# A new global order, new engines and new buffer homes for all 1,263 tasks of a linear-attention and expert-attention kernel

## The chip, the cores and the metric

The kernel runs on one core of one Trainium2 chip. The metric is device time in microseconds (us) of that core, as the median of three runs. The profile comes from one further execution of the same program.

## The reference

Two stages follow each other. The first is linear attention per head with a normalised output; the second is a small mixture of four attention experts on that output.

```python
# stage 1: q, k, v are (8, 8, 576, 64): batch, heads, sequence, head size
kv  = einsum('bhsd,bhse->bhde', k, v)
out = einsum('bhsd,bhde->bhse', q, kv)
rms = sqrt(mean(out * out, axis=-1) + 1e-06)
x   = (out / rms * g_norm)            # regrouped to (8, 576, 512)

# stage 2: 4 experts, 2 chosen per token, head size 64
logits = x @ w_gate                   # (512, 4)
w      = softmax over the two largest logits of a token
for e in range(4):
    q, k, v = x @ wq[e], x @ wk[e], x @ wv[e]
    a  = softmax(causal(q @ k.T / 8))
    ye = a @ v @ wo[e]
    out += (w of expert e, 0 where it isn't chosen) * ye
```

Inputs and output are float32; 28.3 MB of q, k and v are read and 9.4 MB are written.

## The kernel before

The program is a flat list of 1,263 tasks. A task is named by a kind, a batch b (0 to 7) and one or two part numbers: `("sc", 3, 1, 2)` is the third piece of scores of expert pair 1 in batch 3, written `sc.3.1.2` below. Each task calls one small function that issues one to a few dozen instructions. `names()` lists all tasks, `ORDER` is a string with two characters for each task that says in which order they are issued, and `ENGINE` has one letter for each task: A (ScalarE, called ACT), V (VectorE, DVE) or G (GpSimd, POOL), used where a task can run on more than one engine. Every engine takes its own tasks strictly in that order, so the order decides what stands behind what in five queues: TensorE (PE), DVE, ACT, POOL, and the queue of SP that issues nearly all DMAs. Batch 0's v is issued by ACT.

`SLOTS` gives each buffer a home, in the order of first use. There are 8 homes of kind L (a whole k, v, q or turned q of one batch, 9.2 KB in each partition, named `kvq` in the profile), 13 of kind t (`tmp`: raw weights, gate products, x before its transpose, y before its store), and 8 PSUM banks (all named `p` in the profile). A PSUM tile is either one bank (`small`) or a pair of banks (`big`). A task that writes into a home waits for the last reader of the buffer that was there before.

The tasks of a batch b are, in the order in which data flows:

| kind | engine | what it does |
|---|---|---|
| lk, lv, lq (lkr, lvr) | SP | loads of k, v, q (and of the last 64 tokens of k and v). Batches 0 and 1 come in halves of 576 KB; batches 2 to 7 as 1,024 KB each for k and v and eight pieces of 144 KB for q |
| q, then qc | PE, DVE or ACT | transposes of q on PE for batches 0 and 1; for batches 2 to 7 qc is a DVE transpose (L478) |
| kv, kvr, kvc | PE, DVE or ACT | k times v, and its copy out of PSUM into `kvx` |
| kgm, kgr | POOL or DVE, DVE | the gate's columns added to `kvx` (L450, L457) |
| out, oc | PE, ACT or DVE | q times `kvx`, and the copy to `o_sb` |
| sq, red, ln, rs, na, nb, nc | POOL or ACT, DVE, ACT, ACT, DVE, DVE or POOL, DVE | squares (L506, L508), their sum, and 1/rms with a Newton step |
| xm | DVE or POOL | scales `o_sb` by 1/rms into `tmp` (L564) |
| x, xc | PE, ACT or DVE | transposes x into `xT` |
| gl, lg, m8, sh, ex, mk, gt, den, rd, gate | DVE, POOL, ACT | the gate of every token |
| qp, kp, qpc, kpc, v, vc | PE, then ACT or DVE | the projections and their copies |
| sc, exp, msk | PE, ACT, POOL | scores, exponentials (L690), causal mask (L696) |
| pv, rc, iv, oc2 | PE, DVE, DVE or POOL, DVE | a times v, and the scaling |
| ot, otc, y, yc, st | PE, ACT or DVE, PE, ACT or DVE, SP | transpose, the product with wo, copy, store (L781) |

Five prologue tasks belong to batch 0 alone: gg and gb broadcast g_norm and w_gate over the partitions by matmul on PE, g8, g9 and wg scale them on DVE; lw, ws and lwo, wo load and scale the weights.

L276 is the one line of a helper through which every matmul goes, and L285 that of every copy, so the profile's groups are told apart by their tiles.

`ZEROS` asks for matmuls of zeros (`p<-zeros`) ahead of a task: they are issued just before it, into the bank that it will write, and are overwritten by it. In the kernel before there are 69 of them at 18 tasks, from batch 0 to batch 7.

Of the kernel before, what the change touches and what calls it, by code (L numbers as in the profile page):

```python
# [20 lines left out]
DIGITS = "0123456789ABCDEFGHIJKLMNOPQRSTUVWXYZabcdefghijklmnopqrstuvwxyz+-"  # L21

ZEROS = {
    ('kv', 0, 1): 9, ('kv', 0, 0): 9, ('out', 0, 0): 6, ('out', 0, 1): 2, ('out', 0, 3): 6,
    ('kv', 1, 1): 3, ('x', 0, 1): 6, ('kv', 2, 0): 2, ('sc', 0, 0, 1): 2, ('y', 0, 3): 2,
    ('out', 2, 3): 6, ('x', 1, 2): 2, ('sc', 1, 1, 0): 2, ('ot', 1, 1): 2, ('ot', 2, 0): 2,
    ('sc', 3, 1, 1): 4, ('x', 4, 1): 2, ('sc', 7, 1, 2): 2,
}

ORDER = (  # L30
    "050104030M02305I00060908072+310c0A0B0e0d0a0G0E0N0b0f0C0T0I2-0V0Y5N0Z0K0S0U0Q0W5P0X0H5K0g0F0w0h0D0i0x0J0k0j0o0l"
    "320p0+0m0-0q0n0s0O130y0L0r5O140t0z7l18340u100R115G19150v1I1J161A1D171K1E1S1L1F1M1T125H1b3C1U0P1P1o7q3D1c2z1p1G"
    "3E1B1C1H1V1d1Q1R5F3F1N1W1Y1u7m1m1v1X1Z1n1O1q1a1e3A1h1r1f7n1g1i2M1j3B1k1l7f1y2N2K1z1s2L1w1t331x5Q2R35242SAA2O38"
    "1+39362527AD28262P5R375T2T1-5S2Q5U295V203G7g3W3H2U3X3I2V2X7j2Y212W3J5L5W222Z2a5X2b5e5M5Y2c3O2f5f3K3P235Z5a2A3L"
    "3Q2C3M2d2D2eA93N2B2E3Y7r2F5J3R7t2G5b7sA47u2H2g3Z2I3S2h2JA62i3T2j7h3U2t2n2u7k3V2q2o7i2k5c3a2r2w2l3b3c2x3d5d2m3e"
    "3h5s5g2s5k3n2y3i3f3j5h3k2v3o2p3g423q3wA35l3p3lAE435m815w3tAC3m7v5n7w5t3x46805i7xCZ445x473r3y7+455y3u5j3s5o5z3v"
    "5u485p4e493z5q7-3+4C3-5r4f7p405v414A4D7y4E5+4B5-CW607z4c4FCV61AF4dAICT62AH65A8AGA54G6E4M4H4J666H7o4K4P636B4Q4N"
    "4gCa4m674L4h4O6C646S6K6D4I6F4i6T4n4S686G6WA76I4U6X4o6Y6J694RAB6Z6L6a4V6A6N4W4T6M6b6O6UCU4X6P6e4Y6Q826RCd4Z726V"
    "6fCe4a8373704bE-6c71776d7478AJ8GAK75Ez794pASChALAT764q8HCiAMEvAQCfCgAR4rE+4jAOAN6jEt4k6gCjCkAP6h4lEy88896i6pEu"
    "6q8A4s6k4t4u4v7D4x6lHR7A8B7E6r7B7F6m4w4y4z6n7C4+844-8C6o85Ex8K8D5686Cl8L6s57598MCb8E7G6u875A537I506v8I8FCm5C54"  # L40
    "6w6t5D51Co7H6xCnAk5B7L8JAU6y7J6z557K6+7M5E8NF36-F57N8OCp8P527O8QCc7PFFF658F48RFECY7c7Z8S7dCX8T7T8b7a7Q7U7W7e8h"
    "7R8c7X8U8V8d7V8iAl7b8w8jCs8YAV7Y8W8k8x7SAc8XAW8eAYEwAdAXAgAeAZ8+F0Ah8ZAfHNAa8fF18a8-8sCr8gAi8u8tAb8y8v8n928lAm"
    "Aj8mF28zAn8o9S938pCtAoHPAp8q90Cq9T8rAqArHQ9QAs91Av94HI9RA-9DF89EF795D0AyHSCyF9D8B5HO9U9VAtFG96HK9FD9Cz9W9XD1B2"
    "9aAu9A9YFH9dFAB89BAzB0HL9Z9eA+9bB69CB1HMB39fC+BIB79cB4BKBJHJB99gD2C-BABM9iBLDA9h9jBNFCHHAw9k979lAxDBCu9m98BB9n"
    "D4BCHh9oCv99BOBDD59pBSCwBEBPFBBFBQD3BTHgBsBRCxFD9HD6BtHf9GBG9L9I9MBq9J9NBH9KBdBUBrBeBaBVBf9OD7BXHe9PHTBWHVBYA0"
    "HUA1BbHWBZA29zDCBc9wDD9+9t9xDE9-BgDFDG9u9qDH9yDPBh9r9vBu9sBlBxDSBiDIBvDQDYHXBjDRHYBmBkBwFIHZDJBnByDkBoDTDVDlFJ"
    "BpDKDUB+DLBzC1FUB-DMFYFVC2C0FZDmDgC3DnHaC4DhDWC6C5DXC7HbFKDNDoC8DOC9DZFQDpHcDaFLFMFRDsFNCAHdFSFWCBEGFOFXDtFPCC"
    "EHDiFTFaDqCDDjFbCNDrCKDbCODcFcCEFdCLDdCHFeCPDeFfDfEECFCICMFgCGFjCQEFCJE1DuFsE2EIDvELFkFhEJCRFmFtFlCSEMFuD+DwEO"
    "EKFiGAD-FpFyFnGBG4EPENFoFqE0G5ERFrDxEQG6DyFzG8FvEUF+ESG9HuEWG7DzHmETHvEXHyE3HnF-EYEVG0HzHoG1E4G2EZFwE6E5G3HpFx"
    "EaE7HiEbH+E8HqHjE9H-GGHrHkHsGCGHHlGgGDHwEAHtEcGhGeEBEdHxECGfGEEDI0I1I2EnI3GFEhI4I7EoEeEiEkEpIAEfEqEjGLElGREgI8"  # L50
    "IDGMEmIBGSIGI9GlGiErIEGjICEsGNIHIJIFIUGmIWIIGkIYIVGTIXGnIaIZI5IKIbI6GIILGrGOGJIMJ6IPINGsGKGPIcGtJ7IgIOGQIdIeIQ"
    "IhIRISITGVIfJ4GZGaGbGUJ5IrGoGWIsGXJ8GpGYItJBGcJ9GqIoGdIlIpJAIiIjIqGuGvGwImGxGyIkJHGzG+JIG-InJCJEJJH0IvJFH1JDIu"
    "IzHBI+IwI-H8JGHCH5H9IxHDJKIyH6H2HAJMJNJLJOH7J2H3J0JSJ3J1HEJPJTH4JQHFJWJRHGJZJXJUJcJaJVJYJfJdJbJiJgJeJjJhJk"
)
ENGINE = (
    "VVVVVVVVVVVVVVVVVGVGVGVGVAVVVVAVVVGVVAVVVVVAAVVAGVVVGVVAAVVVAVAAVGVAAVVVAAVGVAAVGVAAVVVGVVVAVVAVVVGVAVVAVGAVVV"
    "VVVAVVVVVVVAVAVVVAGVAGVAGVAGVVVVVVGVVAVAVAVAGVAGVAGVAGVVVVVVVVVVVVVVAVVAVVAVVVVVVVVVVVVVGVVVVAVAVVVVGVVAAVVAAV"
    "VAGVVVGVAAVGVVVVVAGVAVVVGVAGVAVGAVGVVGVAVVVVVAVVVAVVVAGVAGVAGVAGVVVVVVGVVVVVVAVAGVAGVAGVAGVVVGVVGVVVVVVVAVVVVV"
    "AVVAVVVVVVVVVVVVVVVVVVVVGVGVVVVVVVGVVAAVVVAVVAGVVAAVAAVVVVVVVVGVAVVAVVVVVAVGAVGVVGVVVVVVVVVVVAVVVAGVAGVAGVAGVV"
    "VGVVVVVAVVVAVAGVAGVAGVAGVVVVVVVVVAVAVVAVVAVVAVVAVVVVVVVVVVVVVVVVVVVAVVGVVVVVVVGVVAGVVAGVVAAVVAAVAAVVVVVGVVGVAV"  # L60
    "VAGVAVVAVVAVGVVVVAVAVAVAVVVAVAVAGVAGVAGVAGVVVVVVVVVAVAVAVAGVAGVAGVAGVVVGVVGVVAVAVVAVVAVVAVVVVVVVVVVVVVVVVVVVVV"
    "VAGVGVVVVVVAAVVVGVVAAVVAGVVVAVAAVVVVVVVAVVVVVVGVVVVVVGAVGVVVVVVAVVVVVAVAVAVAGVAGVAGVAGVVVGVVGVVAVVVAVAGVAGVAGV"
    "AGVVVGVVGVVAVVVVAVVAVVVVVVVVVVVVVVVVVVVVVVVVVVGVGVVVVVVAGVVVAVVAGVVVGVVAAVAAVVVVVGVVGVAVVAGVAGVAVGAVGVVVVAVVVA"
    "VAVVVAVAVAGVAGVAGVAGVVVGVVVVVVVAVAVAGVAGVAGVAGVVVGVVGVVAVAVVAVVAVVAVVAVVVVVVVVVVVVVVVVVVVAGVGVVVVVVVGVVAAVVAGV"
    "VVAVVAGVAAVVVVVVVVGVVGVAVVVGVAVGAVGVVGVVVAVAVVVVVAVAVAGVAGVAGVAGVVVGVVVVVVVAVAVAGVAGVAGVAGVVVVVVVVVVVVVVAVVAVV"
    "AVVAVVVVVVVVVVVVVVVVVVVAGVGVVVVVVAGVVAGVVAAVVVAVVAAVAAVGVGVVVAVVVVVVVVVGVVVVAVGVVVVAVVVVVAVVVVVAVAGVAGVAGVAGVV"
    "VGVVVVVAVAVAVVVAGVAGVAGVAGVVVVVVGVVVVVVVVVAVVAVVVVVAV"
)
SLOTS = (
    "010234015236012314750627803120913A22B2C36200304552320205104011023183104071301322002311010412213426176A9B213C11"  # L70
    "0125630381523143501142237025031B304C100016740A6714231430140131120314476091303300321305013504231530485611231200"
    "10706017BC0A6797830605716230234503121301141223B217000412330145675161001230323203021403002110310504A563C0189112"
    "B0112016772104345110010033203451001065712A862203C20309B6217260123237031211340010202230212627143320502631A3C238"
    "21B032617201340113021120120613210023411514902371000154203240130A55C"
)


# [45 lines left out]
def kernel(  # L123
# [15 lines left out]
    B, H, S, Dh = q.shape  # L139
# [29 lines left out]
    def big(*key):  # L169
        n = place(("bg",) + key)  # L170
        touched.append((n, (0, 1)))
        return pairs[n]
# [6 lines left out]
    def small(*key):  # L179
        n = place(("sm",) + key)  # L180
        touched.append((n // 2, (n % 2,)))
        return pairs[n // 2][:, n % 2, :]

    def buf(key, shape, dtype, name):
# [23 lines left out]
    n = Dh // NCH  # L208
    nc.gpsimd.tensor_copy(
        out=pick[:].rearrange("p (r x) -> p r x", x=n), in_=ident_f[0:n, 0:n].unsqueeze(1).to_broadcast([n, P // n, n])  # L210
# [64 lines left out]
    def mm(*args, **kwargs):  # L275
        done.append(nc.tensor.matmul(*args, **kwargs))  # L276
# [500 lines left out]
    def store(b, qc):  # L777
# [7 lines left out]
        kv=kv, kvr=kv_rest, kvc=kv_copy, q=q_tr, qc=q_copy, kgm=kvg_mul, kgr=kvg_sum,  # L785
        out=out_mm, oc=o_copy, sq=square, red=red, ln=ln, rs=rs, na=newton_a, nb=newton_b, nc=newton_c, gl=gl, lg=lg, xm=xm, x=x_tr, xc=x_copy,
        m8=m8, sh=sh, ex=ex, mk=mk, gt=gt, den=den, rd=rd, gate=gate, v=v_mm, vc=v_copy,
        qp=lambda b, pr: proj("q", b, pr), kp=lambda b, pr: proj("k", b, pr), qpc=q_proj_copy, kpc=k_proj_copy,
        sc=sc, exp=exp, msk=msk, pv=pv, rc=rc, iv=ivm, oc2=o_scale, ot=ot, otc=ot_copy, y=y_mm, yc=y_copy, st=store,
# [66 lines left out]
    PE_TASKS = ("gg", "gb", "kv", "kvr", "q", "out", "x", "v", "qp", "kp", "sc", "pv", "ot", "y")  # L856

    def zero_matmuls(n, count):
        if n[0] in ("x", "v", "y", "ot"):
            t = small(*n)  # L860
        else:
            key = {"qp": ("q",), "kp": ("k",), "q": ("qt",)}.get(n[0], (n[0],)) + n[1:]
            if n[0] in ("kv", "kvr"):
                key = ("kv", n[1], n[2] if n[1] == 0 else 0)
            t = small(*key) if n[0] in ("kv", "kvr") and n[1] not in NINE else big(*key)[:, 0]
        lo = NCH * Dh if n[0] in ("kv", "kvr") else 0
        fresh = n[0] not in ("kv", "kvr") or n[1] not in opened
        for _ in range(count):
            mm(t[:, lo:], lhsT=zeros[:, 0:P], rhs=zeros[:, lo:512], start=fresh, stop=True, skip_group_check=True)

    with tc.manual_schedule():
        for n in order:
            touched.clear()
            done.clear()
            if n in ZEROS:
                zero_matmuls(n, ZEROS[n])
            emit[n[0]](*n[1:])
            order_banks(n)
# [30 lines left out]
```

## Time and profile before

| what | value |
|---|---|
| median of 3 runs (lowest, highest) | 238.92 us (238.84, 239.56) |
| the profiled execution's own time | 239.94 us |
| its span from first to last instruction | 238.2 us |
| PE busy | 208.1 us (87%), of it 15.8 us matmuls of zeros |
| DVE, ACT, POOL busy | 168.8 us, 138.1 us, 107.6 us |
| mean granted TensorE clock | 0.981 |
| DMA | 40.43 MB, mean 170 GB/s |

The profiled execution lies 1.0 us above the median of the runs, and 1.7 us of its time lie outside its span. PE is the busiest engine by a wide margin. The DMA engines are busy for most of the first 150 us or so and little after that. Busy time of PE is modelled at its end, so it is read here together with the times at which its tasks begin.

### The profile page before, as it was taken

The page shows a single profiled execution, that of the slowest core. Times are in us where ns is not written, and L with a number is a line of the kernel's source. Part 1 is how long each engine was busy: PE and PEld are TensorE (multiplying, and loading weights), DVE is VectorE, ACT ScalarE, POOL GpSimd, SP SyncE. Part 2 cuts the span into 40 slices and gives each one's busy share as a digit, 9 for nine tenths or more (in the row PEclk, how much of TensorE's full clock was granted, in tenths as well). Part 3 has the DMA queues.
Part 4 walks back from the last instruction along what each step waited for, and adds up shares of the span by engine and source line. Part 5 has one row for each costly group of instructions (what it writes and reads, how often), then busy time and mean ns, then how long its engine had stood idle before and what let it go on. Part 6 is the DMA issues. An engine that isn't in the chain of part 4 may idle for free.

```text
span 238.2 us, 8788 instructions
## 1 busy us (share of the span) xinstructions
PE 208.1 (87%) x3713; PEld 170.4 (72%) x3713; DVE 168.8 (71%) x411; ACT 138.1 (58%) x255; POOL 107.6 (45%) x194
## 2 busy tenths in 40 slices
PE   0698789987977998999997997999999899999891
PEld 0276458965935896987674994997898699789550
DVE  2052889343779799756799997996758957786381
ACT  2010346473451655548836887757968877884961
POOL 7104254054537521608846407843794674053510
PEclk9999999999899799999999999999999999999998
DMA  6999899999897969984998999910500500230046
GB/s 222 393 359 309 136 272 220 228 234 242 128 222 226 248 105 224 238 105 95 320 176 189 254 138 221 205 62 12 191 0 3 184 19 6 96 104 3 1 182 218
DMA packets 86280, 40.43 MB, mean 170 GB/s; under 512 B 63952, under 2 KB 78816, under 8 KB 86240
## 3 DMA queue, kind: packets, MB, share of 16 engines
q1 hardware_dynamic: 85600, 38.68, 67.5%
q10 hardware_dynamic: 544, 1.18, 1.3%
q8 instruction: 29, 0.48, 1.0%
q14 instruction: 11, 0.09, 0.1%
q0 software_dynamic: 96, 0.01, 0.0%
HBM read 30.42 MB, written 9.44 MB: 167 GB/s over the span
## 4 chain that ended last, share of the span: by engine, by line
PE 62%; DVE 14%; ACT 9%; issue 5%; DMA 3%; SPq 3%; POOL 2%; DVEq 0%; POOLq 0%; ACTq 0%
PE p L276 61%; ACT PT L690 6%; DVE tmp L564 5%; SPq L347 3%; DMA g_cols<-in_g_norm_dram 3%; DVE ms L512 2%; POOL sq L508 1%; DVE kvq L478 1%; PE p L279 1%; ACT o_sb L285 1%; DMA out_dram<-tmp 1%; DVE tmp L285 1%; DVE gl L549 1%; DVE kvx L457 1%; DVE o_sb L285 1%
## 5 line engine op out<-in xcount | busy, mean ns | idle before, releaser
L690 ACT ACTIVATE PT<-p 128x1024 bf16<-128x1024 f32 (+1 forms) x64 | 50.4, 842 | 15.7 <-PE p L276 14.5
L696 POOL TENSOR_SCALAR_AFFINE_SELECT PT<-PT 128x256 bf16<-128x256 bf16 (+1 forms) x80 | 30.8, 404 | 40.0 <-ACT PT L690 39.3
L508 POOL TENSOR_TENSOR sq<-o_sb 128x512 f32<-128x512 f32 (+1 forms) x20 | 20.7, 1039 | 20.6 <-ACT o_sb L285 8.7
L512 DVE TENSOR_REDUCE ms<-sq 128x8 f32<-128x520 f32 (+1 forms) x40 | 26.8, 678 | 4.4 <-POOL sq L508 3.5
L276 PE MATMUL p<-wv_r,xT 128*128 128x256 f32 x160 | 26.5, 299 | 1.1 <-DVE o_sb L285 0.9
L564 DVE TENSOR_TENSOR tmp<-o_sb,rstd 128x512 fp32r<-128x512 f32 x23 | 26.8, 1251 | 0.2
L450 POOL TENSOR_TENSOR tmp<-kvx,wg_t 128x512 f32<-128x512 f32 x13 | 17.0, 1310 | 21.4 <-DVE kvx L285 19.9
L276 PE MATMUL p<-kvx,kvq 64*64 64x68 f32 x1152 | 25.0, 226 | 1.8 <-DVE kvx L457 1.4
L276 PE MATMUL p<-ident_r,tmp 128*128 128x128 f32 (+1 forms) x160 | 23.2, 276 | 3.4 <-DVE tmp L564 2.2
L564 POOL TENSOR_TENSOR tmp<-o_sb,rstd 128x512 fp32r<-128x512 f32 x17 | 22.0, 1325 | 8.9 <-DVE rstd L543 8.5
L276 PEld LDWEIGHTS p<-kvx,kvq 64*64 64x64 f32 x1152 | 21.9, 136 | 4.8 <-issue 2.9
L276 PE MATMUL p<-qTp,kT 64*128 64x64 f32 (+4 forms) x192 | 23.1, 342 | 2.5 <-DVE o_sb L285 1.6
L276 PEld LDWEIGHTS p<-ident_r,tmp 128*128 128x128 f32 x160 | 20.5, 191 | 6.4 <-DVE root L530 1.6
L276 PE MATMUL p<-kvq,kvq 64*64 64x64 f32 (+1 forms) x768 | 23.5, 226 | 1.1 <-issue 1.1
L276 PEld LDWEIGHTS p<-kvq,kvq 64*64 64x64 f32 (+1 forms) x768 | 20.8, 139 | 4.3 <-issue 3.9
L276 PEld LDWEIGHTS p<-wv_r,xT 128*128 128x128 f32 x160 | 21.5, 195 | 2.5 <-DVE o_sb L285 1.0
L276 PEld LDWEIGHTS p<-qTp,kT 64*128 64x128 f32 x192 | 14.4, 185 | 8.5 <-issue 2.6
L276 PE MATMUL p<-vext,PT 128*128 128x65 bf16 x480 | 19.6, 196 | 1.1 <-issue 0.5
L285 ACT COPY o_sb<-p 128x544 f32<-128x544 f32 (+1 forms) x26 | 15.3, 612 | 8.9 <-PE p L276 7.7
L276 PEld LDWEIGHTS <-PT 128*128 128x128 bf16 x480 | 17.1, 99 | 3.9 <-issue 0.7
L285 ACT CAST xT<-p 128x512 fp32r<-128x512 f32 (+1 forms) x23 | 12.0, 532 | 13.6 <-PE p L276 13.5
L276 PE MATMUL p<-zeros 128*128 128x512 bf16 (+1 forms) x69 | 15.8, 351 | 4.5 <-ACT PT L690 3.5
(93 smaller groups left out, 356.6 us busy)
## 6 DMA issues: line engine op xcount, KB each, us to landing
out_dram<-tmp SPq DMA_DIRECT2D x32, 256.0 KB, 2.4
kvq<-in_q_dram SPq DMA_DIRECT2D x48, 144.0 KB, 5.7
kvq<-in_v_dram SPq DMA_DIRECT2D x6, 1024.0 KB, 8.3
kvq<-in_k_dram SPq DMA_DIRECT2D x6, 1024.0 KB, 7.2
kvq<-in_q_dram SPq DMA_DIRECT2D x4, 576.0 KB, 7.2
kvq<-in_k_dram SPq DMA_DIRECT2D x4, 576.0 KB, 8.8
kvq<-in_v_dram ACTq DMA_DIRECT2D x2, 576.0 KB, 6.8
kvq<-in_v_dram SPq DMA_DIRECT2D x2, 576.0 KB, 8.7
```

Source lines behind the costliest of these rows:

```text
L276: done.append(nc.tensor.matmul(*args, **kwargs))
L279: done.append(nc.tensor.transpose(*args))
L285: rd_(nc.scalar.copy(dst, src) if engine[task] == "A" else nc.vector.tensor_copy(out=dst, in_=src))
L347: nc.sync.dma_start(long("q", b)[r * 32 : (r + 1) * 32, c0 * S : (c0 + 2) * S].rearrange("p (x d) -> p x d", d=32), q[b, h0 : h0 + 2, :, ( ...
L450: ew(("kgm", b, m)).tensor_tensor(out=short("g", b, m)[:].rearrange("p (e f) -> p e f", e=E), in0=kvx[b % 2][:, m, E : E + 2 * Dh].unsquee ...
L457: nc.vector.tensor_reduce(gates_of(kvx[b % 2])[:, m], tiles["t", "g", b, m][:].rearrange("p (e k d) -> p k e d", e=E, k=2), axis=AX_X, op= ...
L478: nc.vector.transpose(t[:, i * S : (i + 1) * S], tiles["L", "q", b][:, i * S : (i + 1) * S])
L508: nc.gpsimd.tensor_tensor(out=dst, in0=src, in1=src, op=AluOpType.mult)
L512: nc.vector.tensor_reduce(mss[b % 2][:nt, i, :], sqs[(NB * b + i) % 3][:nt], axis=AX_X, op=AluOpType.add)
L564: ew(("xm", b, i)).tensor_tensor(out=short("x", b, i, dtype=FP32R)[:].rearrange("p (c m k r) -> p m k r c", c=NCH, m=NCH, k=2), in0=ob[:, ...
L690: rd_(nc.scalar.activation(PT[:, :, d0 : d0 + o], big("sc", b, pr, j)[:, :, 0:o], ACTF.Exp, scale=scale))
L696: nc.gpsimd.affine_select(out=d, in_=d, compare_op=AluOpType.is_ge, fill=0.0, base=0, pattern=[[0, 2], [1, w]], channel_multiplier=-1,)
```

## The change

`ORDER`, `ENGINE`, `SLOTS` and `ZEROS` are replaced. The tasks and their instructions are the same, as are the numbers of homes (but for `gl`, which has one home in place of two); 186 of the 1,263 tasks go to another engine, and nearly every task stands at another place. In the diff the strings are cut to their first and last lines.

```diff
 ZEROS = {
-    ('kv', 0, 1): 9, ('kv', 0, 0): 9, ('out', 0, 0): 6, ('out', 0, 1): 2, ('out', 0, 3): 6,
-    ('kv', 1, 1): 3, ('x', 0, 1): 6, ('kv', 2, 0): 2, ('sc', 0, 0, 1): 2, ('y', 0, 3): 2,
-    ('out', 2, 3): 6, ('x', 1, 2): 2, ('sc', 1, 1, 0): 2, ('ot', 1, 1): 2, ('ot', 2, 0): 2,
-    ('sc', 3, 1, 1): 4, ('x', 4, 1): 2, ('sc', 7, 1, 2): 2,
+    ('q', 0, 1): 10, ('kv', 0, 0): 2, ('kv', 0, 1): 3, ('out', 0, 0): 8, ('out', 0, 3): 8,
+    ('q', 1, 1): 8, ('kv', 2, 3): 8, ('out', 1, 4): 6,
 }
 ORDER = (
-    "050104030M02305I00060908072+310c0A0B0e0d0a0G0E0N0b0f0C0T0I2-0V0Y5N0Z0K0S0U0Q0W5P0X0H5K0g0F0w0h0D0i0x0J0k0j0o0l"
...
+    "04050c0e0100030d020S06070f090A2+0T0U0V320B0Y0I0a0Z0C0b0W0X0g0E2z2-0k5F310h5H0w0x0o0l080m0p305G0s0n0M0y0z1I0q1J"
...
 ENGINE = (
-    "VVVVVVVVVVVVVVVVVGVGVGVGVAVVVVAVVVGVVAVVVVVAAVVAGVVVGVVAAVVVAVAAVGVAAVVVAAVGVAAVGVAAVVVGVVVAVVAVVVGVAVVAVGAVVV"
...
+    "VVVVVVVVVVVVVVVGVGVVVGVVVVVAVVVAVVVVVAVVVAVAAVVAAVVVAVVAAVVVAVAAVGVAAVGVAAVGVAAVGVAAVVVVVVVAGVAGVAVVVGVVVGAVGV"
...
 SLOTS = (
-    "010234015236012314750627803120913A22B2C36200304552320205104011023183104071301322002311010412213426176A9B213C11"
...
+    "00112326041501223046172011523620072123130483261500194A1513120B071320123854530148730301456A97021670211103018430"
...
 )
@@
     def zero_matmuls(n, count):
-        if n[0] in ("x", "v", "y", "ot"):
+        if n[0] in ("x", "v", "y", "ot", "gg"):
             t = small(*n)
```

Decoded, the change reads as follows.

The start of SP's queue, before and after:

```
before: lq.0.1 lq.0.0 lw.v.1 lk.0.1 lv.1.1 lvr.2 lk.0.0 lv.1.0 lq.1.0 lw.k.0 lw.q.1 lw.q.0 lw.k.1 lk.1.1 lq.2.4
after:  lq.0.0 lq.0.1 lk.0.0 lk.0.1 lv.1.0 lq.1.1 lw.k.1 lw.q.0 lw.q.1 lk.1.0 lk.1.1 lk.2.0 lq.1.0 lkr.2 lv.1.1 lv.2.0
```

The start of PE's queue, before and after:

```
before: gg gb q.0.1 q.0.2 q.0.0 kv.0.1 kv.0.0 out.0.0 out.0.4 out.0.1 out.0.2 out.0.3 kv.1.1 x.0.1 q.1.1 v.0.1 x.0.4
after:  q.0.1 q.0.2 kv.0.0 gg gb kv.0.1 q.0.0 out.0.0 out.0.1 out.0.4 out.0.2 out.0.3 kv.1.0 q.1.1 kv.1.1 kv.2.3
        q.1.2 q.1.0 x.0.4 out.1.4 kv.2.2 out.1.0 out.1.2 x.0.0
```

The tasks that change engine most often, as the number on each engine:

| kind | before | after |
|---|---|---|
| xm | DVE 23, POOL 17 | DVE 5, POOL 35 |
| kgm | DVE 3, POOL 13 | DVE 8, POOL 8 |
| sq | ACT 20, POOL 20 | ACT 25, POOL 15 |
| yc | ACT 29, DVE 11 | ACT 20, DVE 20 |
| vc | ACT 17, DVE 23 | ACT 23, DVE 17 |
| gl, nb | POOL 2 and 5, DVE 6 and 7 | POOL 6 and 10, DVE 2 and 2 |

The matmuls of zeros number 53 instead of 69. All of them stand ahead of tasks in the first twenty or so of PE's queue; ten stand ahead of PE's very first task. The branch for "gg" in `zero_matmuls` is not used by the new `ZEROS`.

In PE's queue the stages of a batch lie further apart: the y products of batch 0 stood together after ot.0.1, and now four and more stages of other batches lie between the first and the last of them.

## The prediction

> **What bounds the kernel now.** I read the page first (busy shares, then the slices), then the engines' sums by stretch, then PE's timeline, then the groups by form.
>
> ```profile
> span 238.2 us, 8788 instructions
> ...
> PE 208.1 (87%) x3713; PEld 170.4 (72%) x3713; DVE 168.8 (71%) x411; ACT 138.1 (58%) x255; POOL 107.6 (45%) x194
> ...
> PEclk9999999999899799999999999999999999999998
> DMA  6999899999897969984998999910500500230046
> ```
>
> PE is the bound; DVE follows, and POOL is the least used. The DMA row is the second thing to see: the transfers are near full until about slice 26 (155 us) and then almost stop. So up to there the order of the loads can hold PE back, and behind it only PE and its partners count. The sums by stretch (busy us of PE, PEld, DVE, ACT, POOL with instruction counts, then granted clock, DMA share, GB/s) say where PE loses time:
>
> ```profile
> 0.00:26.00 26.00, 15.38 (x324) 10.36 (x325) 8.41 (x25) 2.48 (x3) 8.86 (x24) 1.00 0.98 313
> 26.00:35.00 9.00, 7.90 (x233) 5.10 (x233) 7.71 (x19) 4.98 (x16) 3.36 (x4) 1.00 0.92 188
> ...
> 50.00:78.00 28.00, 22.22 (x505) 16.29 (x502) 19.18 (x38) 12.43 (x21) 15.57 (x21) 0.94 1.00 213
> ...
> 157.00:200.00 43.00, 42.22 (x748) 36.56 (x747) 33.13 (x84) 33.14 (x60) 25.82 (x47) 1.00 0.16 57
> ```
>
> From 157 to 200 us PE has no room. In 0 to 35 and 50 to 78 us it has: there much of its "busy" is zeros or waiting. PE's timeline (start, us, what, idle before and its releaser) shows both:
>
> ```profile
> 6.83 0.66 PE L276 MATMUL p<-g_row,one_row 1*128 1x64 f32 x2 [6.83 <-DMA g_row<-in_g_norm_dram]
> ...
> 9.21 3.68 PE L276 MATMUL p<-o_sb,one_row 1*64 1x512 f32 x8
> ...
> 12.82 4.12 PE L276 MATMUL p<-ident_f,kvq 64*64 64x64 f32 x144
> ...
> 26.00 1.17 PE L276 MATMUL p<-kvx,kvq 64*64 64x68 f32 x48 [1.41 <-DVE kvx L457]
> ```
> ```profile
> 57.34 0.30 PE L276 MATMUL p<-qTp,kT 64*128 64x64 f32 x2 [1.57 <-DVE o_sb L285]
> ...
> 75.98 0.61 PE L276 MATMUL p<-zeros 128*128 128x512 bf16 x2 [0.68 <-ACT xT L285]
> 76.24 0.74 PE L276 MATMUL p<-ident_r,tmp 128*128 128x128 f32 x4
> 77.86 0.74 PE L276 MATMUL p<-wv_r,xT 128*128 128x256 f32 x4 [0.88 <-DVE o_sb L285]
> ```
>
> The first out product of batch 0 starts at 26.0 us. The later waits are for a PSUM bank that a copy has yet to empty: x.1.2 is issued right behind x.1.0 into the bank that xc.1.0 still reads.
>
> **A ledger.** For each kind of task I took from the timeline the median time from its start to the next task's start where PE doesn't idle (out 0.53 us, x 0.49, v 0.55, a projection 1.06 to 1.14, pv 0.37 and 0.56, y 0.43, one q transpose of batches 0 and 1 0.86). All tasks of PE add up to 185.4 us; this is the same in both orders. The lag of a task is its start less the PE work queued ahead of it. Before, it is 15.0 us at out.0.0, 20.1 at x.0.1 (35.0 us), 26.2 at kv.3.0 (63.6), 29.9 at out.2.3 (72.4), 34.2 at kp.1.1 (84.7), and 48.1 when PE ends (233.5). Another 4.7 us for the last copy and store close the span. So 34 us of lag come up in the first 50 us of PE work and 13.9 in the other 135.
>
> **Part 1: the start.** Before, PE begins with gg and gb, whose small loads land late, and the three q transposes, which need both halves of q (landed by 9.3 us in the trace), wait for them until 12.8. After, q.0.1 is first: about 9.4. At 1.56 us each (the rate of these at 12.8; the same 48 matmuls took 0.93 us at 35.6) q.0.1 and q.0.2 end at 12.5. lk.0.0 now follows lq.0.1 at once, where lw.v.1, lk.0.1, lv.1.1 and lvr.2 stood ahead of it; halves landed about 1.7 us apart, so it lands near 11 instead of 15.3. Two zeros (0.4) and kv.0.0 (1.3 to 1.7) bring us to 14.5, gg 0.5 to 15, gb 1.8 to 3.6 to 17 to 18.6, three zeros and kv.0.1 to 19 to 20.3. The gate's columns follow on DVE: kgm 0.7 to 0.98 and kgr 0.67, twice each, all four now in DVE's queue, with q.0.0 and eight zeros beside them on PE: 2.7 to 3.3 us. out.0.0 starts between 21.5 and 23.5; I take 22.5, 3.5 us earlier.
>
> **Part 2: the loads.** SP's queue runs ahead of PE until a home is missing, and the homes of k, v and q in the new order are each freed 1 to 35 us of PE work before their next load, so the transfers set the pace. Spacing of landings in the full stretch: a half 1.7 us, 256 KB 0.8, a 1,024 KB load 3.8, a pair of rests 0.7, a 144 KB piece 1.0. Up to lk.2.0 before: 2.3 + 12 x 1.72 + 8 weights 6.4 + two rests 1.4 + 7.6 + six pieces 6 = 44.3, and it landed at 48.0; so a factor of 1.08. After, lv.2.0 has ahead of it 2.3 + 20.6 + 3 x 0.8 + 7.6 + 0.7 = 33.6, or 36.3 with the factor. kv.2.3 needs it and has 17.0 us of PE work ahead: lag 16.6 to 19.3. The new queue goes on with kv.2.3 strictly, so everything behind (x.0.4 first) waits with it; the zeros ahead of q.1.1, kv.2.3 and out.1.4 fill such waits and cost nothing while these last, 22 x 0.22 = 4.8 us if the data were early. Next, out.2.2 needs the last piece of q.2: 55.7 by the same sum, 60.2 with the factor, two DVE transposes of 0.76 more: 61.7, with 39.5 us of PE work ahead: lag 22.2. Before, the lag at that amount of work was 26 to 28, and by 50 it was 34. Further down the loads gain on PE (lv.5.0 at 93 for a kv.5 due at 95; lv.7.0 near 134 for a kv.7 due about 144).
>
> **Part 3: the dense stretch.** Two things in the order speak for fewer waits. PE work between the last write to a bank and the next task's write to it is under 0.5 us for 11 tasks before (among them x.1.2 and sc.3.1.1, which start 0.93 and 2.09 us after the task ahead of them) and for one after; under 1 us, 41 against 19. And the PE work between a batch's last out and its first x is 3.9 us at batch 1 before, and at least 9.6 for batches 1 to 7 after. Against it: homes of kind t are reused with as little as 0.3 us of PE work between release and reuse (3.6 at least before), some behind stores.
>
> The engines' sums hardly change the bound. From the groups:
>
> ```profile
> L564 DVE TENSOR_TENSOR tmp<-o_sb,rstd 128x512 fp32r<-128x512 f32 x23 | 26.8, 1251 | 0.2
> L564 POOL TENSOR_TENSOR tmp<-o_sb,rstd 128x512 fp32r<-128x512 f32 x17 | 22.0, 1325 | 8.9 <-DVE rstd L543 8.5 <-PE p L276 0.4
> ```
>
> DVE: 18 xm less (-22.5), 9 yc (+6.1), 5 kgm (+3.5 to 4.9), 2 oc and 2 qpc (+2.9), vc, gl, nb, qc and small ones (-6.5): about 152. POOL: 18 xm (+23.9), 5 kgm less (-6.6), 5 sq less (-5.2), gl, nb and small ones (+5): about 125. ACT about -2. All lie beside PE's 185; what matters is only who stands behind whom.
>
> **The clock: a rule and a row.** Zeros end at PE work 20; before, they reach to batch 7. [...] Each drop lasted 3.4 us at half clock and made the tasks in it 1.3 to 1.7 us longer. I follow the row: without zeros 0 to 4 drops, 226 to 232, and take 2 as before: no change. That the change does what its first ten zeros seem meant for, a PE that is fast at its first task, I doubt: the start's transposes ran at 0.6 of the later rate, at half rate ten zeros of 0.43 us end near 5.6, and q.0.1 comes at 9.4. Worth 0 to 1.3 us; I take 0.
>
> **The sum.** Lag of 22.2 at 39.5 us of work, then the loss rate of the old late stretch (13.9 over 135, so 15.0 over 146) gives 37.2 at the end; bank waits gone (-3), tighter t homes and unseen queue waits (+4): 38.2. Span 185.4 + 38.2 + 4.7 = 228.3, 9.9 below 238.2. The profiled execution lies 1.0 above the median, so from 238.92: 229.
>
> **Rivals.**
> Denser still (0.13): after 40 us of work PE loses only 6 to 9, as the bank spacing allows: lag 30, span 220, time near 221. For: 157 to 200 us runs so already.
> Loads slip (0.17): kv.2.3 stands in PE's queue for a 1,024 KB load that took 8.3 us from issue to landing before (v, median); if the order of packets or clock drops put 4 to 6 us on the early lag, only the start and a little remain: 234 to 238.
> Slower (0.12): POOL's queue. Five scalings a batch at 1.33 (1.83 at worst) stand in one queue with ten masks at 0.43 (1.25 at worst). From the last out to the first x it takes 0.72 + 1.04 + 0.68 + 0.48 + 0.8 + 0.78 + 1.33 = 5.8 us against 9.6 of cover: 3.8 to spare. If masks and scalings hold POOL for more than that ahead of xm, each us beyond costs 8 us over eight batches; 1.7 beyond is 13.6 and the kernel ends near 243. Against: POOL is idle for 39 us waiting for exponentials before.
> No gain (0.03): these just cancel. The likeliest (0.55) is 224 to 234.
>
> **The numbers.** 229; 220.5 to 238 leaves out about one in twenty below and three in twenty above. Faster by over 0.3% (about what a measurement of this kernel can tell): 0.85; same 0.03; slower 0.12.
>
> **What would show it.** Right: out.0.0 at 21.5 to 23.5; lv.2.0 landing at 34 to 37 with kv.2.3 right behind; out.2.2 near 62; DMA row falling off before slice 26; few waits of PE above 1 us after 65 us; POOL busy near 125. Wrong: kv.2.3 after 40; PE waiting for `tmp` from POOL in every batch; PEclk under 9 in more than three slices past the start; SP waiting for stores before the last load.

## The result and the profile after

The changed kernel takes 222.23 us (median of four runs, 220.71 to 225.86), the kernel before 239.24 us beside it (238.84 to 239.69): a ratio of 0.927 with an interval of 0.919 to 0.935, or about 17 us. The ratio leaves out executions that ran over 1.5% longer than the fastest of their kernel; the medians and ranges here and below have all of them. The forecast was 229.0 us with a range of 220.5 to 238.0. The profiled execution of the changed kernel took 220.71 us, with a span of 219.0 us. The lines of its page that answer to those of before:

```profile
span 219.0 us, 8779 instructions
...
PE 201.9 (92%) x3697; PEld 168.7 (77%) x3697; DVE 151.6 (69%) x392; ACT 137.5 (63%) x253; POOL 111.2 (51%) x215
...
PEclk9676988999999999999999999999999999999996
DMA  5999997696999799979899984992001021922277
```

PE is still the bound. From slice 8 (38 us) on every digit of the clock row but the last is a 9. The DMA row falls off in slice 28 (148 to 153 us). The sums by stretch (busy us of PE, PEld, DVE, ACT and POOL, then clock, DMA share, GB/s):

```profile
0.00:26.00 26.00, 20.00 (x438) 13.23 (x439) 7.81 (x26) 5.18 (x7) 4.56 (x20) 0.80 0.97 335
26.00:35.00 9.00, 6.08 (x117) 3.62 (x116) 5.80 (x15) 4.23 (x15) 1.88 (x4) 0.81 1.02 255
50.00:78.00 28.00, 27.01 (x512) 25.00 (x510) 21.34 (x59) 20.57 (x40) 17.61 (x29) 1.00 0.92 201
157.00:200.00 43.00, 43.00 (x589) 37.68 (x588) 32.08 (x87) 32.95 (x60) 24.90 (x53) 1.00 0.24 84
```

Read the third row against the same row of before: 27.0 of 28 us instead of 22.2. Read the second row too: PE does *less* in 26 to 35 us than before (117 matmuls instead of 233), and the reason for that was not in the prediction. The clock of the first row is not to be set against that of before: the trace of before has no record of the clock ahead of 17.4 us, and the view prints 1.00 there, but its q.0.2 started a matmul every 25.4 ns (from 14.2 us), just as that of the changed kernel did (from 10.3 us), whose record says half clock.

The prediction's ledger, taken from the timelines of both kernels (lag in us of the first task behind so many us of PE work), says where the time came from:

| PE work queued ahead, us | 11 (out.0.0) | 20 | 30 | 50 | 100 | 140 | end |
|---|---|---|---|---|---|---|---|
| before | 15.0 | 20.5 | 22.1 | 34.2 | 40.3 | 43.6 | 48.1 |
| after | 11.4 | 24.2 | 26.0 | 26.1 | 27.1 | 28.3 | 29.1 |

The lead of 3.6 us at out.0.0 is gone at 20 us of work and has become a delay of 3.7 us. Between 20 and 50 us of work the kernel before loses 13.7 us and the changed one 1.9; from there to the end 13.9 against 3.0. So 11.8 + 10.9 - 3.7 = 19.0 us. PE's timeline of the start (start, us, what, idle before and its releaser):

```profile
6.26 0.58 PE L274 MATMUL p<-ident_f,kvq 64*64 64x64 f32 x24 [1.36 <-DMA kvq<-in_q_dram]
9.58 2.20 PE L274 MATMUL p<-ident_f,kvq 64*64 64x64 f32 x72 [2.74 <-DMA kvq<-in_q_dram]
...
22.41 0.62 PE L274 MATMUL p<-kvx,kvq 64*64 64x68 f32 x25
23.66 1.77 PE L274 MATMUL p<-kvx,kvq 64*64 64x68 f32 x87 [0.62 <-issue]
...
30.82 1.91 PE L274 MATMUL p<-kvq,kvq 64*64 64x64 f32 x72 [2.92 <-issue]
...
38.34 0.69 PE L274 MATMUL p<-kvq,kvq 128*64 128x64 f32 x16
38.96 0.69 PE L274 MATMUL p<-ident_f,kvq 64*64 64x64 f32 x31
40.77 1.17 PE L274 MATMUL p<-ident_f,kvq 64*64 64x64 f32 x65 [1.13 <-issue]
```

And PE's waits over the whole span (for what, us in total, times, longest), of before and then of the changed kernel:

```profile
PE p L276 <- ACT PT L690: 4.5, 8, 1.1
```
```profile
PE p L274 <- issue: 6.0, 5, 2.9
PE p L274 <- DMA kvq<-in_q_dram: 4.1, 2, 2.7
...
PE p L277 <- ACT tmp L283: 0.7, 1, 0.7
PE p L274 <- ACT OT L283: 0.4, 1, 0.4
PE p L274 <- DVE o_sb L283: 0.3, 1, 0.3
```

The waits for a copy or an exponential, 4.5 us for `PT` alone before, are nearly gone. What is left besides the first load is "issue": PE stands still while no semaphore, no data and no bank that the profile shows holds it.

**What "issue" is here.** The five gaps end at 23.66, 30.82, 40.77, 51.50 and 92.15 us. Counted over all of PE's records behind its opening drain (matmuls, weight loads and the semaphore instructions between them), the instruction behind each gap is number 705, 961, 1473, 1985 and 3521: always 449 plus a multiple of 256. The trace also has 29 DMA packets of 16 KB of kind "instruction" on queue q8, and the span has 29 such borders. Sixteen KB over 256 instructions is 64 bytes each. Worked out from the DMA records of the changed kernel (us):

```
block of PE instructions  entered   next packet begins   landed   next block's first runs   gap before it
449                        17.50          21.10           22.23         23.66                 0.62
705                        23.66          28.29           29.41         30.82                 2.92
961                        30.82          32.33           34.38         36.16                 -
1217                       36.16          37.93           39.34         40.77                 1.13
1729                       45.38          48.19           50.06         51.50                 0.99
6337                      169.77         170.30          171.23        176.44                 -
```

By these times each packet brings the next block, and begins at about the time when the running block was entered, or later. From 9 to 55 us, with a DMA share of 0.95, it begins 2.9 us after the entry (median of eight, 1.5 to 4.6) and takes 1.4 us; from 155 us, with a DMA share of 0.30, it begins 0.3 us after it (seven, -0.4 to 1.7) and takes 1.0. The block can be used some 1.4 us after its landing, with every gap within 1.41 to 1.55. A block in the full stretch thus takes up to 7.2 us, and the 72 matmuls of 64*64 of a kv task and their weight loads use 144 of its 256 instructions in 1.3 us. In this trace no packet lands before the block ahead of its own has been entered: one block runs, and the next is on its way or has come.

### The profile page after: what moved, and what is told of

Same layout as the page of the kernel before. It is cut to its first block, busy times and chain, and to the rows that moved or that the text cites. A ratio compares the mean times of both kernels' runs of the same rounds, so it can differ in the third digit from the quotient of the medians.

```text
span 219.0 us, 8779 instructions
## 1 busy us (share of the span) xinstructions
PE 201.9 (92%) x3697; PEld 168.7 (77%) x3697; DVE 151.6 (69%) x392; ACT 137.5 (63%) x253; POOL 111.2 (51%) x215
## 4 chain that ended last, share of the span: by engine, by line
PE 87%; DMA 4%; issue 4%; POOL 2%; ACT 1%; DVE 1%; SPq 0%; POOLq 0%
PE p L274 84%; DMA kvq<-in_q_dram 4%; PE p L277 2%; POOL tmp L562 1%; ACT PT L688 1%; POOL PT L694 1%; DVE o_sb L283 0%; ACT tmp L283 0%; SPq L309 0%; DVE tmp L283 0%; ACT OT L283 0%; POOL inv L729 0%; POOL g_gt L608 0%; POOLq L562 0%
## 5 line engine op out<-in xcount | busy, mean ns | idle before, releaser
L562 POOL TENSOR_TENSOR tmp<-o_sb,rstd 128x512 fp32r<-128x512 f32 x35 | 37.9, 1116 | 4.7 <-PE p L274 3.1
L274 PE MATMUL p<-kvq,kvq 64*64 64x64 f32 (+1 forms) x768 | 25.1, 242 | 2.9 <-issue 2.9
L506 POOL TENSOR_TENSOR sq<-o_sb 128x512 f32<-128x512 f32 (+1 forms) x15 | 15.5, 1037 | 22.7 <-ACT o_sb L283 11.5
L274 PEld LDWEIGHTS p<-kvq,kvq 64*64 64x64 f32 (+1 forms) x768 | 22.4, 154 | 5.7 <-issue 3.9
L534 POOL TENSOR_TENSOR root<-root,ms 128x40 f32<-128x40 f32 (+1 forms) x10 | 2.7, 273 | 40.4 <-DVE root L528 40.4
L274 PE MATMUL p<-qTp,kT 64*128 64x64 f32 (+4 forms) x192 | 22.5, 341 | 0.0
L274 PEld LDWEIGHTS p<-ident_r,tmp 128*128 128x128 f32 x160 | 20.6, 191 | 2.1 <-issue 0.4
L274 PE MATMUL p<-wo_b,OT 128*128 128x512 bf16 (+1 forms) x96 | 21.0, 348 | 0.4 <-ACT OT L283 0.4
L274 PE MATMUL p<-xT,wq_r 128*128 128x288 f32 x128 | 20.1, 299 | 0.0
L274 PE MATMUL p<-xT,wk_r 128*128 128x288 f32 x128 | 19.8, 299 | 0.0
L283 DVE COPY o_sb<-p 128x544 f32<-128x544 f32 (+1 forms) x16 | 11.4, 718 | 10.5 <-PE p L274 6.7
L504 ACT ACTIVATE sq<-o_sb 128x512 f32<-128x512 f32 (+1 forms) x25 | 15.8, 632 | 4.3 <-DVE ms L510 2.4
## 6 DMA issues: line engine op xcount, KB each, us to landing
kvq<-in_k_dram SPq DMA_DIRECT2D x4, 576.0 KB, 10.3
```

The costliest lines, as they stand in the source:

```text
L283: rd_(nc.scalar.copy(dst, src) if engine[task] == "A" else nc.vector.tensor_copy(out=dst, in_=src))
L504: nc.scalar.activation(dst, src, ACTF.Square)
L506: nc.gpsimd.tensor_tensor(out=dst, in0=src, in1=src, op=AluOpType.mult)
L534: ew(("nb", b, g)).tensor_tensor(out=roots[b % 2][:, cols], in0=roots[b % 2][:, cols], in1=ms[:, cols], op=AluOpType.mult)
L562: ew(("xm", b, i)).tensor_tensor(out=short("x", b, i, dtype=FP32R)[:].rearrange("p (c m k r) -> p m k r c", c=NCH, m=NCH, k=2), in0=ob[:, ...
```

## The experiments

The changed kernel is the base unless it is said otherwise. Ratios are to the kernel before, run beside each.

**1. What the later zeros cost.** The first question was why kv.1.0 and everything behind it came 4 us late.

```diff
 # no_late_zeros
 ZEROS = {
     ('q', 0, 1): 10, ('kv', 0, 0): 2, ('kv', 0, 1): 3, ('out', 0, 0): 8,
-    ('out', 0, 3): 8, ('q', 1, 1): 8, ('kv', 2, 3): 8, ('out', 1, 4): 6,
 }
```

> The changed kernel without the zeros ahead of out.0.3, q.1.1, kv.2.3 and out.1.4 (30 matmuls of zeros less; the ten, two, three and eight of the start stay). Theory A, these zeros delay PE: they stand where data is there already (kv.2.3 starts at 38.3 us, its loads landed by 32.8), so x.0.4 moves from 41.9 us to about 37.5, out.1.4 from 43.8 to about 39, and the time falls by 3 to 5 us, to about 218. Theory B, they only fill waits for loads and for copies: nothing moves, 221 to 223. Rival on the clock: without them PE falls to half clock more often between 25 and 50 us and the time stays or rises by up to 3 us. Theory on instruction fetch: the idle gaps of PE that nothing releases end about 1.4 us after a 16 KB packet of instructions lands and lie 256 PE instructions (or a multiple) apart; with 60 instructions taken out ahead, they move to other tasks, at the same counts of instructions.

222.76 us (218.49 to 224.38), ratio 0.917 (0.907 to 0.928). With 30 zeros less the lag at 20 us of work is 24.9 instead of 24.2. The 30 matmuls and their weight loads are 60 instructions, so if a border is what stops PE, other tasks must stop, at the same counts. They did: the gaps lie at 29.59 (4.38 us, count 961), 35.75 (2.47, count 1217) and 40.83 us (0.56, count 1473), and two more further down (69.06 and 129.14 us, counts 2497 and 4801). The time that the zeros had filled became waiting: x.0.4 began at 42.2 us, not at 37.5 as theory A has it. By the ratios alone a gain of some 2 us is not excluded, as the intervals overlap. (In this trace PE ran at half clock from 27.4 to 47.9 us, so its times aren't set against the others; the counts can be.)

**2. No zeros at all.**

```diff
 # no_zeros, and once more no_zeros_again
-ZEROS = {...}
+ZEROS = {}
```

> The changed kernel without any zeros. Against the run without late zeros alone: if the zeros at the start keep PE's clock up, q.0.1 to out.0.0 run slower (out.0.0 later than 22.4 us by 1 to 3 us) and the end with them; if they only fill waits, out.0.0 stays at 22 to 22.5 and the time is that of the run without late zeros. Clock drops after 50 us: none, as PE has no idle stretch there, whichever theory holds.

220.01 us (218.77 to 227.98), ratio 0.919 (0.913 to 0.925). PE's timeline has four stalls in the same blocks:

```profile
23.30 3.33 PE L273 MATMUL p<-kvx,kvq 64*64 64x68 f32 x94 [0.60 <-issue]
...
30.32 0.89 PE L273 MATMUL p<-kvq,kvq 64*64 64x64 f32 x41 [2.72 <-issue]
...
36.05 1.35 PE L273 MATMUL p<-kvq,kvq 64*64 64x64 f32 x50 [2.50 <-issue]
...
40.74 0.56 PE L273 MATMUL p<-ident_f,kvq 64*64 64x64 f32 x18 [2.02 <-issue]
```

These are counts 705, 961, 1217 and 1473, now 7.8 us in all against 6.0, and the stalls cut tasks in the middle: 41 of the 72 matmuls of a kv task stand behind one of them. PE ran at half clock in 17.3 to 27.5, 30.9 to 34.3 and 41.2 to 48.0 us, and the lag at 20 us of work is 24.0, against 24.2 in the changed kernel, which between 17 and 48 us was at half clock in 17.6 to 21.0 and 31.2 to 34.6 us alone. The longer time at half clock did not make the lag longer here.

Run again beside the changed kernel:

> The changed kernel itself, beside the next one on the same chip: 221 to 224, and 0.92 to 0.935 of the kernel before.

> The changed kernel without any zeros again, beside the changed kernel on the same chip. If the zeros cost time, it is 1 to 3 us faster, about 220; if PE's instruction packets set the pace of the first 45 us in both, the two lie within 1 us.

220.57 us (219.19 to 221.61), ratio 0.927 (0.921 to 0.933), for the changed kernel and 219.69 us (218.94 to 224.59), ratio 0.922 (0.916 to 0.928), without zeros. The intervals overlap, though both pairs lie 1 to 2 us on the side of no zeros. The 53 zeros bring nothing that these runs can tell, and a kernel without them is the simpler of two equals.

**3. The first ten zeros.**

```diff
 # no_first_ten
 ZEROS = {
-    ('q', 0, 1): 10,
     ('kv', 0, 0): 2, ...
```

> The changed kernel without the ten zeros ahead of PE's first task alone. The prediction's term: they end long before q's second half lands at 9.5 us, so 0 us and at most 1.3 us later; 222 to 224. If they do what they seem meant for, the q transposes and kv.0.0 take longer without them and the time rises by 2 us or more.

221.44 us (220.34 to 222.18), ratio 0.926 (0.920 to 0.932). They bring 0 us, as the prediction took: with and without them the matmuls of q.0.2 start 25.4 ns apart. In the changed kernel the clock rose in 3.9 to 7.3 us after them and was at half again in 7.3 to 14.2, when q.0.1 and kv.0.0 ran.

**4. The start's order.** gg and gb ahead of q.0.1 again, as before, with the rest of the new order behind.

```diff
 # gg_gb_first: start of PE's queue; five PSUM pairs get other homes for it
-    q.0.1 q.0.2 kv.0.0 gg gb kv.0.1 q.0.0 out.0.0
+    gg gb q.0.1 q.0.2 kv.0.0 kv.0.1 q.0.0 out.0.0
-    ('q', 0, 1): 10
+    ('gg',): 10
```

> The changed kernel with gg and gb ahead of q.0.1 in PE's queue, as before the change (the ten zeros stand ahead of gg; five PSUM pairs of the first seven tasks have other homes). If the new start is worth its lead, out.0.0 goes from 22.4 us to 25 to 26 and the end is 2.5 to 3.5 us later, about 225. If loads or instruction fetch set the pace after it, kv.1.0 and what follows keep their times, and the time stays within 1 us of 222.

223.35 us (221.44 to 224.63), ratio 0.934 (0.927 to 0.940): between the two expectations, 1 to 2 us above the changed kernel with overlapping intervals. out.0.0 comes 2.4 us later (lag 13.8), but at 20 us of work only 0.6 us of it is left (24.8):

```profile
27.01 1.76 PE L280 MATMUL p<-kvx,kvq 64*64 64x68 f32 x86 [1.57 <-issue]
...
33.89 1.27 PE L280 MATMUL p<-kvq,kvq 64*64 64x64 f32 x70 [2.56 <-issue]
```

Counts 705 and 961 again. Most of what the new start wins is given back by the second border. Over all twelve runs of the new order, here and below, out.0.0 begins anywhere from 21.1 to 25.3 us, but kv.2.2, the first task behind 20 us of work, always from 43.7 to 45.5.

**5. Order, engines and homes apart.** `ENGINE` can be exchanged without the order; `SLOTS` follows the order of first use, so the homes stay with their order here.

```diff
 # new_order_old_engines
-ENGINE = ("VVVVVVVVVVVVVVVGVGVVVGVV...   # of the changed kernel
+ENGINE = ("VVVVVVVVVVVVVVVVVGVGVGVG...   # of the kernel before
 # old_order_new_engines: the kernel before, with the reverse exchange
```

> The changed kernel with the old choice of engine for every task; order, homes and zeros are the new ones. Theory, the order makes the dense stretch: DVE gets about 16 us of work back and the queues no longer fit exactly, so the time rises by 2 to 6 us, 224 to 228, still far from 239. Rival, the engines make it: most of the gain goes, 233 or more.

> The kernel before with the new choice of engine for every task; order, homes and zeros are the old ones. Theory, the order makes the dense stretch: between -2 and +3 us against the kernel before. Rival, the engines make it: faster by 5 us or more. The prediction's rival of a POOL that binds: with 35 xm on POOL and the short way from out to x of the old order, the x matmuls wait for POOL and the time rises by 5 us or more.

The first took 252.37 us (249.45 to 257.15), ratio 1.053 (1.041 to 1.066), the second 247.04 us (244.85 to 249.19), ratio 1.032 (1.020 to 1.045). Both are slower than the kernel before, so the theory that the new order (with its homes) alone makes the dense stretch has fallen. The expected waits of x for POOL did not come either: under the old order with the new engines PE waits for POOL's `tmp` once, for 0.9 us. The ledger shows what each part does:

| lag at PE work, us | 20 | 50 | 100 | 140 | end |
|---|---|---|---|---|---|
| before | 20.5 | 34.2 | 40.3 | 43.6 | 48.1 |
| old order, new engines | 20.6 | 33.3 | 42.1 | 47.8 | 54.4 |
| new order, old engines | 23.7 | 28.4 | 39.8 | 47.1 | 59.0 |
| after (both new) | 24.2 | 26.1 | 27.1 | 28.3 | 29.1 |

Between 20 and 50 us of work the order does most: 4.7 us lost with the new one under old engines, 12.7 with the old one under new engines. Behind 50 it is neither alone: 30.6 and 21.1 us are lost where the matching pairs lose 13.9 and 3.0. The new order under the old engines waits for many partners a little; no single one carries it:

```profile
PE p L274 <- issue: 3.4, 3, 2.9
PE p L274 <- DVE kvq L476: 2.9, 3, 1.3
PE p L277 <- DVE osc L736: 2.8, 3, 1.3
PE p L274 <- ACT PT L688: 2.8, 4, 1.1
```

**6. The homes of the one-bank PSUM tiles.** Order and engines are those of the changed kernel; only the bank of each `small` tile is drawn anew.

```diff
 # small_homes_redrawn: 105 of 145 one-bank tiles move, at random
 # small_homes_lru: 70 of 145 move, each to the bank unused for longest
-SLOTS = ("00112326041501223046172011523620072123130483261500194A15...
+SLOTS = (...the digits of these tiles alone)
```

> The changed kernel with the PSUM homes of the one-bank tiles redrawn at random among those that are free; order and engines are the new ones. Tasks that write a bank less than 1 us of PE work after its last write number 53 in place of 19 (41 in the kernel before), under 0.5 us 26 in place of 1 (11 before). Theory, bank homes carry part of the dense stretch: PE waits for copies out of PSUM in dozens of places, 4 to 10 us slower, 226 to 232. Rival, homes don't matter beside the order: within 2 us of 222.

253.37 us (250.30 to 258.64), ratio 1.062 (1.047 to 1.077): 31 us lost, far above what was expected. PE's waits lie where a bank is reused:

```profile
PE p L274 <- ACT PT L688: 6.0, 8, 1.5
...
PE p L274 <- ACT OT L283: 2.6, 3, 1.4
PE p L274 <- DVE o_sb L283: 2.1, 3, 1.3
PE p L274 <- ACT xT L283: 1.7, 3, 0.8
```

`PT`, `OT`, `o_sb` and `xT` are what ACT and DVE make of a bank that PE wants again. In the changed kernel one task has under 0.5 us of PE work between the last write to its bank and its own; here 26 have. 31 us by 25 tasks is about 1.2 us each. The ledger shows less: of the 29.8 us by which PE falls behind the changed kernel, 21.5 are lost at these 26 tasks, on average 1.05 us where the bank was written by the task just ahead (15 tasks) and 0.5 us at the others (11); 5.0 more lie at tasks with 0.5 to 1 us of work between. The next run tested the price with six such tasks in place of one:

> The changed kernel with the one-bank tiles' PSUM homes drawn anew by a rule that looks at the order alone: the free bank that has been free longest (70 of 145 tiles move). Under 0.5 us of PE work between the last write of a bank and the next stand 6 tasks in place of 1, under 1 us 24 in place of 19. Theory, each such task costs about what the random draw showed (31 us for 25 more of them, 1.2 us each): 5 more cost about 6 us, 226 to 230. Rival, the new schedule fits only its own homes and any change upsets the queues: 240 or more. Second rival, only tasks that follow at once on the same bank cost: within 2 us of 222.

227.14 us (225.69 to 228.14), ratio 0.955 (0.948 to 0.961): 5 us above the changed kernel by the medians and 7 by the ratios, for five more tasks. In the ledger 4.7 of the 6.1 us lie at the six tasks, again 1.05 us at each of the three with no work between and 0.5 at each of the other three. That smaller price held; the 1.2 had the losses elsewhere in it. "Longest unused", which counts turns in the queue, is a worse rule than the homes of the changed kernel; that it would do better if it counted work is not shown.

**7. Which of the 186 moved tasks.** Of these the scalings by 1/rms, xm, weigh most in DVE's queue.

```diff
 # xm_old_engines: the letters of 22 xm tasks as before, all else as changed
-xm: DVE 5, POOL 35
+xm: DVE 23, POOL 17
```

> The changed kernel with the engine of xm alone as before (22 tasks differ: 20 go back to DVE, 2 to POOL); all else is new. If the loss of the old engines (30 us for 186 tasks) comes from DVE's load, these 22 tasks of 1.1 to 1.25 us carry most of it: 235 to 250. If it comes from any task that stands in another queue than the order was made for, they carry their share by number, about 4 us, 224 to 228.

235.14 us (233.99 to 236.04), ratio 0.988 (0.980 to 0.995). Against the 0.927 of the changed kernel that is 0.061 of 239 us, some 14 us, where all 186 tasks cost 0.126, or 30 us, under the new order. The groups and PE's waits:

```profile
L562 DVE TENSOR_TENSOR tmp<-o_sb,rstd 128x512 fp32r<-128x512 f32 x23 | 27.2, 1205 | 0.0
...
L562 POOL TENSOR_TENSOR tmp<-o_sb,rstd 128x512 fp32r<-128x512 f32 x17 | 20.4, 1207 | 4.5 <-PE p L274 3.1
```
```profile
PE p L274 <- DVE tmp L562: 3.1, 3, 1.4
...
PE p L274 <- DVE xT L283: 2.7, 1, 2.7
PE p L274 <- DVE kvq L476: 2.1, 2, 1.2
```

DVE's idle time ahead of its xm is 0.0: they came out of a queue that was full (as it was for the five of the changed kernel), and not only x waits for them (`tmp`), but also, it seems, what needs the copies to `xT` and the transposes of q (`kvq`, L476) in the same queue. By the ledger 8.1 of the 15 us lost lie at the x products and 2.9 at one v that waits for `xT`; some 2 lie at the start, where the clock was at half from 8.8 to 22.5 us. That is over three times the share by number; whether DVE's load or the place in its queue makes it, this run does not separate. DVE is busy for 168.3 us here and 151.6 in the changed kernel; both look harmless as shares (72% and 69%).

**8. Fewer transfers beside the instruction packets.** k of batch 0 gets another home, so that the load of batch 2's k waits for kv.0.1.

```diff
 # loads_held: one digit of SLOTS, the home of kind L of k of batch 0
-2
+7
```

> The changed kernel with k of batch 0 in home 7 instead of home 2, so that the load of batch 2's k waits until kv.0.1 has read batch 0's k (about 19 us instead of 12.7), and all later loads behind it in SP's queue. Theory, the transfers in flight delay PE's instruction packets: with fewer of them between 20 and 25 us the packet that ended the wait at kv.1.0 lands earlier, the 2.9 us gap at count 961 falls under 1.5 us, while batch 2's loads land some 5 us later, at 38, which kv.2.3 just bears: 219 to 222. Rival, a packet takes its time whatever else moves: the gap stays 2.5 to 3 us and the later loads cost up to 4 us, 222 to 226.

222.46 us (221.89 to 223.08), ratio 0.936 (0.931 to 0.940). lk.2.0 was issued at 18.47 instead of 12.69 us, but other data filled the engines: 334 and 344 GB/s in the two halves of 22 to 30 us, where the changed kernel has 322 and 350. The packet came 4.4 us after the block was entered, and the stall stayed. A new wait came for the load behind it:

```profile
29.31 1.28 PE L274 MATMUL p<-kvq,kvq 64*64 64x64 f32 x72 [2.65 <-issue]
...
36.49 1.28 PE L274 MATMUL p<-kvq,kvq 64*64 64x64 f32 x72 [1.59 <-DMA kvq<-in_v_dram]
```

So this run did not lighten what it meant to lighten and decides nothing. That packets begin late while DMA is full is measured (2.9 us after the entry at a DMA share of 0.95, 0.3 us at 0.30); that fewer transfers at that time would shorten the stall stays open.

## Why the prediction was right or wrong

The direction and the range held. Its likeliest case did not: the rival that it gave 0.13, "denser still" with a lag of 30 and a time near 221, is what happened (29.1 and 222.2). That its number fits is in part luck: it had 22.2 and 6 to 9 more, the run has 25.9 and 3.2 more.

**Part 1, the start.** out.0.0 was to start at 22.5 and did at 22.41; q.0.1 at 9.4, and its larger half began at 9.58. The ten zeros at nothing: right. What failed is what came behind it: the 3.5 us were carried forward in the ledger as a gain, and they were given back before 20 us of work, because PE reached the end of its instructions sooner. The twelve runs of experiment 4 say the same: 4.3 us of spread at out.0.0, 1.8 at kv.2.2.

**Part 2, the loads.** lv.2.0 landed at 32.78 us (33.6 to 36.3 was forecast) and the last piece of q.2 at 59.55 (60.2), so the sum of spacings was good. "The transfers set the pace" was wrong, though: kv.2.3 did not follow its load but ran at 38.34, 5.6 us behind it, and out.2.2 at 65.41 instead of 61.7. The lag of 22.2 at 39.5 us of work was in truth 25.9. The DMA row was to fall off before slice 26 and did in slice 28: the last load landed at 148.2 us. The term left out is PE's own instruction blocks: two gaps of 0.62 and 2.92 us and the filled time around them. The zeros, costed at nothing while data were late and at 4.8 us if they were early, cost about nothing for this other reason.

The prediction also misread a row. It took the gap of 1.57 us at 57.34 of before, put down to a copy (`o_sb`), for a wait for a PSUM bank. The task there has count 1985, and the packet had landed at 55.91, 1.43 us ahead of it: the same border.

**Part 3, the dense stretch.** Here is the mis-sized term. "The loss rate of the old late stretch", 15.0 us over 146 of work, with 1 on top for homes and queues, made 16.0; measured were 29.1 - 25.9 = 3.2 (PE runs through 157 to 200 us without a gap). The two signs it named in the order were the right ones (11 tasks under 0.5 us of bank cover before, one after), and so, nearly, was the size: the eleven tasks lose 5.7 us against the ledger in the trace of before, 3.8 of them behind 50 us of work, where the prediction took 3. What it left in was the rest. PE's waits of before from 78 us on:

```profile
PE p L276 <- ACT PT L690: 3.5, 6, 1.1
PE p L276 <- DVE tmp L564: 2.2, 3, 1.1
PE p L276 <- DVE o_sb L285: 0.9, 1, 0.9
```

With smaller ones these are 8.1 us, against 1.7 in the changed kernel, and zeros filled more: about 5 us of before's late loss lie at tasks with 0.5 to 1 us of bank cover, two of them x products that wait for an xm of DVE (0.66 and 1.06 us). The changed kernel still has some 20 tasks with so little cover and loses 1.5 us at them, so the copies now come in time. The rate was carried over from an order that had these waits to one that had them no more; and the 22.5 us that DVE was relieved of were called "beside PE", where experiment 7 gives them up to 14 us in this order. How the late gain divides between banks and engines is not shown: each was measured with the other already in place. Errors of +3.7 early and -12.8 late make -9.1 in the lag, and with a tail of 4.4 instead of 4.7 the span is 219.0 instead of 228.3.

**The clock.** The drop of before at 58.4 us in the sums by stretch:

```profile
55.00:60.00 5.00, 3.43 (x43) 2.21 (x40) 2.54 (x5) 2.32 (x3) 2.06 (x4) 0.84 1.12 263
60.00:65.00 5.00, 5.00 (x165) 4.79 (x164) 3.55 (x10) 2.17 (x4) 2.88 (x3) 0.82 0.82 119
```

It came behind 3.4 us in which PE worked 54% of the time, with a longest gap of 1.57 us; the one at 78.9 us behind 3.4 us with 59% and a longest gap of 0.88 us. That the new order has two drops as well was an estimate that no run shows: in the changed kernel none came behind 35 us until PE was done (215.5 us). At 1.3 to 1.7 us each, the two of before are about 3 of the 11.8 us won between 20 and 50 us of work, which the prediction did not count. The changed kernel has PE at 96 to 100% in the rows shown from 50 us on. Its first 35 us do have drops: the one at 31.2 us follows 3.4 us in which PE worked 14% of the time, with a longest gap of 2.92 us, but the one at 17.6 us follows 3.4 us in which PE was busy throughout. What takes the clock down is not shown.

**The rivals of the other side.** POOL's queue was to hold up xm: no wait of PE for POOL is in its list of waits, and the one copy behind a late xm of POOL cost PE 0.26 us (at 150.2 us). POOL was to be busy for 125 us and was for 111.2; 8 of the 14 us are its xm, which took 1,116 ns instead of the 1,325 of before.

## What to carry to other kernels

Do not carry a loss rate from an old schedule to a new one: price the kinds of wait it is made of (here 1.05 us for each task that writes a bank just after the task ahead wrote it, 0.5 us where less than 0.5 us of work lies between), count them in both orders, and add. Order, engines and homes of an in-order, five-queue schedule are one thing: the new engines without the new order and homes were 9 us slower than the kernel before, the new order and homes without the engines 14 us slower, and all together 17 us faster. Where the profile says "issue" ahead of an engine, or names a releaser that had long been done, count the engine's instructions up to the gap, semaphore instructions too, and look for an instruction packet that landed just before it; the start of many small matmuls at a DMA share of 0.95 was held up by that here, for 2.92 us at the longest gap, and 2.4 us at out.0.0 were worth 0.6 us at 20 us of work, and the ten zeros ahead of the first task 0 us.

## What the runs showed of the hardware that was not expected

- PE's instructions come in blocks of 256 by DMA, one ahead: the packet began 2.9 us (median, 1.5 to 4.6) after the block ahead of it was entered at a DMA share of 0.95, 0.3 us at one of 0.30, and could be used about 1.4 us after it had landed. Twelve runs of the new order, with 0 to 53 zeros and two starts, have a lag of 23.5 to 25.3 us at 20 us of work.
- A matmul of zeros stands in the same blocks as the others: taking 30 away moved the stalls to other tasks at the same counts and left x.0.4 where it was (42.2 instead of 41.9 us).
- The scaling xm is faster on both engines when DVE has few of it: 1,116 ns on POOL and 1,103 on DVE with five on DVE, 1,207 and 1,205 with 23 in the same order, 1,325 and 1,251 in the kernel before. Why is not shown.
